# Sigmoid attention with two feed-forward layers: the last 64 keys of two pairs of heads as four 64x64 products

## The chip, the cores and the metric

One core of a Trainium2 chip runs the program. The metric is the time of one execution on the device in microseconds (us). TensorE is called PE below and its weight loads PEld; VectorE is DVE, ScalarE ACT, GpSimd POOL, SyncE SP.

## What is computed

```python
def _attn_ref(q, k, v):                      # 4 batches, 12 heads, 448 positions, 64 per head, float32
    scores = np.matmul(q, k.transpose(0, 1, 3, 2)) / np.sqrt(64) - np.log(448)
    return np.matmul(1.0 / (1.0 + np.exp(-scores)), v)
# x = heads joined: 1792 rows of 768
def _moe_ref(x, w_gate, w_val, w_out, rms_g):   # d_ff 1536
    xn = x / np.sqrt(np.mean(x * x, axis=-1, keepdims=True) + 1e-06) * rms_g
    g = xn @ w_gate
    return g / (1.0 + np.exp(-g)) * (xn @ w_val) @ w_out
def _moe2_ref(x, w_in, w_out):                  # d_ff 2048
    h = x @ w_in
    return (h - np.tanh(h)) @ w_out
```

There is no softmax: each score goes through a sigmoid by itself, so keys can be handled in chunks in any order.

## The kernel before

**Attention.** The 48 heads are worked on as 24 pairs (`b`, `p`): the two heads of a pair lie on partitions 0 to 63 and 64 to 127. The 448 keys of a pair are cut into chunks of 128, 128, 96 and 96 (`rows_of`, `LAST` = 96). For each chunk and head, a product of 64 rows by the chunk's keys by 448 queries gives scores in a PSUM bank (`scores`, L771, plain float32, in the first two pairs; `split_scores`, L751, in the other 22, where q and k are split into a high and a low part by `split_qk` and each product is made of three). ACT takes the sigmoid of each bank (L778). Then `pair_av` (L801) multiplies values by sigmoids: one product per chunk and head, both heads into the two halves of one bank, float32. `pair_end` copies that bank and squares it for the norm. A plain float32 product stands twice in the trace, since it is two instructions there.

**Loads.** `pair_load` fetches a pair's q and k by SP's queue (L694, and two pieces of 64 rows for the last 64 keys, L699, in batches 0 and 1) and v by POOL's or SP's queue (L706, four pieces in batches 0 and 1, three in 2 and 3). Pairs are loaded three ahead.

**Feed-forward.** After attention come the products of the two layers (L1133, L1078, L1158): 128x128 weights against 448 columns, most of them by a scheme that makes seven block products out of eight. Weights are converted on ACT and DVE on the way (L439, L511, L522), partly during attention, and partial sums are added in DRAM (L956).

**What sets the order.** Each piece of work is put on record by `add` with its engines, its costs and the tiles it reads and writes. `Plan.lay` then lays all pieces out: among those that could start soonest by the planner's costs it takes the one with the lowest rank in `ORDER`, a table of numbers, one per piece. Work of one stream ("attention", "moe", "norm") keeps its own order on PE. Buffers come from pools whose sizes stand in `Plan(...)`; PSUM has 8 banks ("at" for scores, up to 2 "av" for values). At the very start PE runs `N_WARM` products of zeros (L446) before its first real one.

Of the kernel before, what the change touches and what calls it, by code (L numbers as in the profile page):

```python
# [244 lines left out]
0bw0aJ0OG1J61Od0kW1LG1vP0000g12UZ0tR1Ts35c17J1Zr0Bn2nY1Wy2OF25P1lm1M01012RL05315n0ou0hJ0aK0jP19B18p1EC0lE1He0nC0Yf0zx0Ck
1Rt1NH20500N0yJ0Dk09O09C0kR24g0Me2FM2B61SX0nw08s04V1J10JK0VG0xW00016D2bp0cI1n-0BK2Bv0570Cy0001p41y_0UI19F0v-1qc1qQ1UD1jS
1aZ0Ws1e80000ra0001Te1pa00016X0000Oq21s27y2zJ1ZZ0xU1AZ1gH0es0Ht1p80K10S40v80uf0Fp0I418v2gN1qX24K2F12v111e2KU28g20H0Z40Jy
0Ft03-15r03c0gr0bG1Kr1w42CI18b0J40cM0fs1Oz0000m80Qa1911h51cX1lz1nt1PT1xA2e91T62721uW1wo0tW0vf00M0va05S0FB2fQ3t_2uM1dw1oM
0qD24G1Bl11x22S1GL3iy20Y3nC1Mr19j1Pa2Tm1ih3NK2DH2ou1Gr20A0ud02u3Pz1Ba2TC3343151ao29v0Mm26D01e0xj2y33lP2rD1iU34Z4Aa1-B1wx
30m2ni3ZA2IL2w922w0z31xL1Ip1BN1G-29r2mz2zc2yW0iI21O2hq2bX2-l3Df1XP1pI1Hw2E52Du2T70in1e03lt1_M2nB1f61vf2jg0_R0xf49Z2pU2MD  # L250
1sX2B52Q32E-2VN1en12v1Qk1wF1x02bh2vd2oD24k0qm0YO0cy0zA0kH1mS1zb3Fj2yE3PC2nn38k2rm2fd1Wp1Vp17M1Pv2kQ2KF3MU2-Y3Bj2St37z1vS
3GT3fP2En1XF11001l07x0Q43FU2s63mp42f3KJ1y02921n02b12wD2ke0vO06K0Qj01l1Rt3XV3P32ub4G64kj2Tl30H2L41s_2Ft0yM3iF4Oe42C1kh1vq
3xd2aV0Al0pi15p1eQ0vr0i91_W01l11Z57u5Iu3eW2va3Fv3hh22A27w2Co2B21y61aT28Y0mx0BQ2bE15I0mn56v4xy3ym4Qx4Fg2CU1mJ1yf2fT38o261
4Tk4tm4HF2Rv34t1em1G90TI1tX2ru1JD5MS2kv4S34i741j4yZ58m2w43062DW1xk33J2LM1RG2JQ3B91dG3f34Ea5CH4Iu2Rv3vD3wP2RC1qs2HM3d33y1
35O56y5Fj3vM2x_3Wz3AA2cn1hs2dx2D52A-2Fi1PN2CC2d30o75V85AR4jb4vD5Vd1tH2CX1vH2Vq2ak3302dA2ls2kr5hI4ye5K630_3k83jT3Z-3Oz5zF
4ja50W54i5DF5-y3po3Py3y12QV2tK2fs1wn2C839s2JF2ZC22H2KC3_J4uI5mQ5QD5XM31A3o04B84zn34f2C02mn2Ii3Iy1zn0cx2gs2bw3pW33q3Pb2_B
33040a2vf3F_2j-3IK2m631m1jS33V2n934z3W23G73K43JV3ME4TQ3Q62lp4uS46F32K3dP3mH3wb4FL4Cu5ti57_3Gm3bh2_-2Nj3PV3HD35d2wY3He4Cv
2_63q14p12nm39-3eB46G3f82zT39B30G3Mp4rU4b15HH5cK3vA4Cw4Vy4id59F5Dm4k053f5WE4Xs4532lB3NX3f146S4LG4W_4Cb3HF6MD4ml61C3NU48A
4BC49a3Tu4dR4dg4uv5cU5Vw4sQ5JN3xn4NP4Ce5BF5Lc6WP4Wd4ySAUT61o5zG2_p4e92093k14jE6HI5I24it4cr57s5FE3sV5yp3ph4nw4zQ5-y5Zk4B7
4oi5O75Yt5L957X5-c4f44yG51F4xx5eh4wM4oq5n85bq5qp67p5DO5oG4Q-5SM4VZ4zF5Wh4ru4S-3Hz4x36C65kL62P7In5c06ga5kR5Ny4NQ4Tb4bM6ZL  # L260
5_u6pQ4sj5MK51c50b5hG7M25cW6q45ln5Ba4lhBRP5WV55r5Eb5-v5dw5yr5916jF6Oz5G36S95Hz6aH6W55q06vl6534ss68d6K_5_z6bi6Jj78u6pp6zj
6fs6QQ7g24vb6AV7Fq6mJ5ky78g6cG6qW5vS6XC7MT7Ft6se7oD5qf7Ks6NF62y56b51p6uB6M_6RO7C_6rm6Fm6c57dd80t4Wu6iH8566pA7bN7PQ7is6zS
6nL7Wq8Ok7967217ma6mK7Gr73s7io6pO7sj8tI7iT7RQ7oo7Cm5xB7td73V8VJ6Xg72T7Kc8IK6-s6-F74g7qM9Sv8n68eq6_E76i7rj6_18b96Rl7nb8KU
7-r7ji8Bs8pX7zc85e8c675B7HY97E66U78l8lI7Mh6fm8aZ8uD7za9O39h88Af6kj6nd5yQ6uw8Po8Cw6cS8it7Od7Hq89y7g39FJ9qz7Vi7Aq7lf7xI6wW
# [1117 lines left out]
```

## Time and profile before

| what | value |
| --- | --- |
| median of 3 runs | 1048.71 us (1043.16 to 1049.61) |
| profiled execution | 1046.03 us |
| its span in the profile | 1044.3 us |
| PE busy | 1031.6 us, 99% of the span |
| ACT busy, DVE busy | 687.3 us, 793.4 us |
| bytes moved | 245.68 MB |

The span is what the profiler saw between the first and the last instruction; 1.7 us of the execution lie around it. PE's busy time is that of pipelined products whose ends are modelled, so 99% says that PE nearly always had work, not that it worked at its peak.

### The profile page before, as it was taken

What the parts mean: (1) busy time and instruction counts of PE and PEld (TensorE: products, weight loads), DVE (VectorE), ACT (ScalarE), POOL (GpSimd) and SP (SyncE); (2) the same over time, 40 slices, a digit from 0 to 9 for tenths busy, and PEclk for the clock granted to TensorE, in tenths of its full rate; (3) what the DMA queues carried; (4) which work ended last, traced back from release to release, by engine and by line L of the source; (5) the groups of instructions that cost most, each with busy time, mean ns of one, the idle gap of its engine ahead of it and who ended that gap; (6) DMA issues with size and microseconds to landing.
All of it is one profiled execution on the core that took longest, in us unless ns stands there. A gap on an engine that the chain in (4) does not pass through costs nothing.

```text
span 1044.3 us, 15612 instructions
## 1 busy us (share of the span) xinstructions
PE 1031.6 (99%) x5324; PEld 888.3 (85%) x5324; DVE 793.4 (76%) x1287; ACT 687.3 (66%) x1260; POOL 163.4 (16%) x234
## 2 busy tenths in 40 slices
PE   8999999999999999999999999999999999999998
PEld 3555558999999989999999989999898899999997
DVE  2858988886977996976755866998797878676866
ACT  5877875685775655775663666678575767675742
POOL 4433000000003142201003030000303300003030
PEclk9999999999999999999999999999999999999999
DMA  7897847866959999979549498485959883649492
GB/s 238 287 346 246 298 150 239 302 224 232 305 166 273 326 259 371 326 291 361 169 115 265 148 214 273 162 306 220 234 178 251 262 212 104 229 135 212 124 251 110
DMA packets 102480, 245.68 MB, mean 235 GB/s; under 512 B 16640, under 2 KB 56992, under 8 KB 102400
## 3 DMA queue, kind: packets, MB, share of 16 engines
q1 hardware_dynamic: 77232, 177.23, 49.8%
q0 software_dynamic: 24864, 67.35, 26.1%
q8 instruction: 42, 0.69, 0.3%
q14 instruction: 38, 0.31, 0.1%
q10 hardware_dynamic: 304, 0.10, 0.0%
HBM read 151.44 MB, written 93.19 MB: 234 GB/s over the span
## 4 chain that ended last, share of the span: by engine, by line
PE 85%; issue 9%; DMA 3%; POOL 1%; DVE 1%; ACT 0%; SPq 0%; POOLq 0%; ACTq 0%
PE ps L1133 43%; PE ps L1078 23%; PE ps L801 7%; PE ps L751 5%; PE ps L1158 5%; POOL out L956 1%; DMA out<-unit 1%; DMA part<-in_vp 1%; DMA part<-in_qkt 1%; PE ps L861 0%; PE ps L836 0%; ACT unit L439 0%; DVE part L522 0%; SPq L699 0%; DVE unit L1014 0%
## 5 line engine op out<-in xcount | busy, mean ns | idle before, releaser
L1133 PE MATMUL ps<-unit,part 128*128 128x448 f32 x2520 | 520.2, 365 | 2.4 <-ACT unit L439 2.3
L1133 PEld LDWEIGHTS ps<-unit,part 128*128 128x128 f32 x2520 | 471.4, 187 | 44.4 <-ACT unit L439 4.6
L1078 PE MATMUL ps<-unit,part 128*128 128x448 f32 x1512 | 311.9, 364 | 1.7 <-ACT unit L439 1.2
L1078 PEld LDWEIGHTS ps<-unit,part 128*128 128x128 f32 x1512 | 283.3, 187 | 24.7 <-ACT unit L439 1.5
L522 DVE TENSOR_TENSOR part<-part 128x768 fp32r<-128x768 f32 (+1 forms) x244 | 214.9, 889 | 68.1 <-ACT part L439 59.3
L439 ACT COPY unit<-ps 128x448 f32<-128x448 f32 x297 | 154.0, 536 | 142.3 <-PE ps L1133 44.8
L439 ACT CAST part<-part 128x768 fp32r<-128x768 f32 (+1 forms) x236 | 182.7, 787 | 21.7 <-DVE part L522 5.8
L885 DVE TENSOR_TENSOR unit<-unit 128x448 fp32r<-128x448 f32 x252 | 152.0, 619 | 45.9 <-ACT unit L439 34.4
L439 ACT CAST unit<-unit 128x448 fp32r<-128x448 f32 x254 | 138.8, 568 | 44.8 <-DVE unit L997 15.5
L1014 DVE TENSOR_TENSOR unit<-ps,unit 128x448 f32<-128x448 f32 x168 | 103.7, 621 | 42.8 <-PE ps L1133 21.1
L890 DVE TENSOR_TENSOR unit<-unit 128x448 f32<-128x448 f32 x144 | 86.0, 618 | 12.6 <-DMA unit<-sumB 8.4
L778 ACT ACTIVATE unit<-ps 128x448 f32<-128x448 f32 (+1 forms) x192 | 86.4, 551 | 8.2 <-PE ps L751 4.4
L956 POOL DMA_DIRECT2D sumB<-unit x48 | 42.4, 945 | 289.5 <-DVE unit L1014 210.3
L801 PE MATMUL ps<-unit,part 128*64 128x448 f32 (+1 forms) x384 | 78.7, 546 | 1.4 <-issue 1.1
L511 DVE SCALAR_TENSOR_TENSOR part<-raw,zero 128x768 uint32<-128x768 uint32 x68 | 64.7, 952 | 12.3 <-ACT zero L439 11.7
L439 ACT CAST zero<-raw 128x768 f16<-128x768 bf16 x52 | 56.1, 1078 | 15.0 <-DVE part L511 5.3
L751 PEld LDWEIGHTS ps<-unit 64*128 64x128 f32 (+1 forms) x528 | 45.0, 171 | 22.2 <-issue 15.3
L801 PEld LDWEIGHTS ps<-unit,part 128*64 128x64 f32 (+1 forms) x384 | 25.2, 136 | 42.2 <-issue 32.5
L1158 PE MATMUL ps<-unit,part 128*128 128x448 f32 x288 | 60.3, 365 | 0.7 <-DVE unit L942 0.3
L751 PE MATMUL ps<-unit 64*128 64x448 f32 (+1 forms) x528 | 60.0, 370 | 0.7 <-DVE unit L439 0.7
L956 POOL DMA_DIRECT2D out<-unit x36 | 31.7, 1092 | 177.3 <-DVE unit L1014 163.3
L1158 PEld LDWEIGHTS ps<-unit,part 128*128 128x128 f32 x288 | 53.7, 188 | 6.3 <-DVE unit L942 1.2
(51 smaller groups left out, 487.6 us busy)
## 6 DMA issues: line engine op xcount, KB each, us to landing
raw<-in_w_out POOLq DMA_DIRECT2D x28, 768.0 KB, 7.9
part<-wD SPq DMA_DIRECT2D x56, 384.0 KB, 5.5
part<-wB SPq DMA_DIRECT2D x36, 384.0 KB, 5.4
wC<-part SPq DMA_DIRECT2D x36, 384.0 KB, 4.7
part<-wC SPq DMA_DIRECT2D x36, 384.0 KB, 3.7
raw<-in_w_in SPq DMA_DIRECT2D x16, 768.0 KB, 7.4
sumB<-unit POOLq DMA_DIRECT2D x48, 224.0 KB, 7.7
wD<-part POOLq DMA_DIRECT2D x28, 384.0 KB, 7.8
```

Of the source, the lines that this page charges most:

```text
L439: add(engines, lambda e: (nc.scalar.copy if e == "ACT" else nc.vector.tensor_copy)(to(), of()), reads, writes)
L522: add({**dve(n, psum=False), **pool(n)}, lambda e: ENG[e].tensor_sub(lo(), of(), hi().bitcast(F32)), [*reads, *kh], [*kl])
L751: nc.tensor.matmul(ps[i, c].tile[:n, :S], lhsT=parts[w].tile[rows, at:at + n], rhs=parts[x].tile[rows, :S], start=q == 0, stop=q == 2)
L778: add(act(S, psum=True), lambda e: nc.scalar.activation(to.tile[at:at + n, :S], ps.tile[:n, :S], AF.Sigmoid, bias=-math.log(S), scale=1.0 ...
L801: nc.tensor.matmul(ps.tile[i * D:(i + 1) * D, :S], lhsT=v.tile[:n, c, i, :] if b < PAIRED else v.tile[:n, i, c, :], rhs=a[c][i].tile[:n, : ...
L885: add({**pool(S), **dve(S, psum=False)}, lambda e: ENG[e].tensor_sub(t["l"].tile, of.tile, t["h"].tile.bitcast(F32)), [of["t"], kh], [kl])
L890: add({**dve(S, psum=False), **pool(S)}, lambda e: ENG[e].tensor_sub(t.tile, x.tile, y.tile), [x["t"], y["t"]], [t["t"]])
L956: add(queue("POOL", True), lambda e: nc.gpsimd.dma_start(out=d.tile, in_=t.tile, accum_op=ALU.add), [t["t"], d["t"]], [d["t"]], moved=move ...
L1014: add(dve(S), lambda e: nc.vector.tensor_add(t.tile, ps.tile[:, :S], t.tile), [ps["t"], t["t"]], [t["t"]])
L1078: nc.tensor.matmul(ps.tile[:, :S], lhsT=part(a), rhs=x[b].tile, start=n in (1, 5) and kp == 0 and q == 0, stop=kp == n_kp - 1 and q == 2, ...
L1133: nc.tensor.matmul(ps.tile[:, :S], lhsT=part(a), rhs=x[b].tile, start=n in ((1, 2, 5) if opening else (1, 5)) and i == 0 and q == 0, stop= ...
L1158: nc.tensor.matmul(ps.tile[:, :S], lhsT=wt, rhs=a[p].tile, start=start and i == 0, stop=stop and i == 2, skip_group_check=True)
```

## The change

The keys are cut into 128, 128, 128 and 64. The three whole chunks go as before (`chunk_scores`, `pair_av`). The last 64 keys of two pairs of heads, four heads, are done together: `tail_scores` makes four products of 64 rows by 64 keys, each in a quarter of PE's array of its own (two row halves by two column halves), into two banks; two sigmoids take these; `tail_av` makes the four 64x64 products of sigmoids and values. The tails are plain float32 in all pairs, not split. A tail's scores stand ahead of the two pairs' other scores, and its values ahead of their other values, so that two "av" banks are open together. `pair_load` makes three transfers a pair (q, k, v), five for the odd pairs of batches 0 and 1, and loads four to five pairs ahead. `N_WARM` goes from 16 to 6. Pool sizes change, and `ORDER` is another table. In the diff the removed lines of functions that are printed above are left out.

```diff
@@ -30,12 +30,12 @@
 PLAIN_SETS = {("B", 0): (2,), ("D", 0): (), ("B", 1): (2,), ("D", 1): ()}
 NQK = S + 4 * P
-LAST = S // 2 - P
+MAIN = S // P
 PAIRED = 2
 SPLIT_QK = (0, 1, 2, 3)
 WHOLE_QK = 2
 HP = H // 2
-N_WARM = 16
+N_WARM = 6
 MM, MM_96 = 203, 190
 SOON = 100
 HELD = 3
@@ -238,127 +238,125 @@
 ORDER = """
-00000000009Q09T00000B0Hv0470000000000000KW04c0mi0DX0Jj01t0470Ih0a10OZ0YV0_0WBFV-c0000PA0Mg1040N802c0Qk05x0Dg0631T50uO1V4
...
-VgQXNrWQ8YMHUlTXZGXeK
+XTM00005G02F0qs09o0L400003D0En1Bv0a50bS0lk0AK0uq0O3XUQXsS0KJ0Og0xM0YP07-1OS0Ja0D915Y0Id0A301415k0R31mU0l40JJ0mI0U11QE0eg
...
 """
@@ -391,10 +389,10 @@
     dram_p = ctx.enter_context(tc.tile_pool(name="spill", bufs=1, space=DRAM))
     plan = Plan({
-        "unit": (N_UNIT, {"moe": N_MOE, "s": 18, "acc": 6, "accs": 12, "st": 4, "sum": 6, "x": 16, "xr": 4, "tmp_m": 8, "tmp_a": 4, "sq": 3, "rstd": 2,
+        "unit": (N_UNIT, {"moe": N_MOE, "s": 22, "acc": 6, "accs": 9, "st": 4, "sum": 6, "x": 16, "xr": 4, "tmp_m": 10, "tmp_a": 4, "sq": 3, "rstd": 2,
                           "xs": 42, "tmp_s": 9, "tmp_x": 4, "qk": 12}),
         "raw": (N_RAW, {"raw": N_RAW}),
-        "part": (N_PART, {"cv": 3, "again": 4, "vs": 4, "qkr": 6, "whl": 6, "op": 8}),
+        "part": (N_PART, {"cv": 4, "again": 4, "vs": 6, "qkr": 10, "whl": 8, "op": 8}),
         "ps": (8, {"mm": 6, "at": 8, "av": 2, "nm": 1, "m2": 8}),
     })
     add = plan.add
@@ -685,125 +683,134 @@
     xs, sqs, rcs, rstd, spilled = {}, {}, {}, {}, {}
     def pair_load(b, p):
...
+        tq, tk, v = qkr_t[b, p] = part_of("qkr", [P, S]), part_of("qkr", [P, 4 * P]), part_of("vs", [P, 4, 2, D] if b < PAIRED else [P, 2, 4, D])
+        vs_t[b, p] = v
         both = qkt[b * H + 2 * p:b * H + 2 * p + 2].rearrange("h r c -> (h r) c")[D:D + P]
...
+        by = "POOL" if b < PAIRED else "SP"
+        def part(e, to, of, key, size, packets=P):
+            add({e: (540 if e == "POOL" else 620, False)}, lambda e: ENG[e].dma_start(out=to(), in_=of), [], [key], moved=moved(size, packets))
+        part("SP", lambda: tq.tile, both[:, :S], tq[0], 4 * S)
+        end = 4 * P if b < PAIRED else S
+        cuts = (0, P, end) if (b, p) == (0, 0) else (0, end)
+        for n, (lo, hi) in enumerate(zip(cuts, cuts[1:])):
+            part("ACT" if hi == P else "SP", lambda lo=lo, hi=hi: tk.tile[:, lo:hi], both[:, S + lo:S + hi], tk[n], 4 * (hi - lo))
+        if b >= PAIRED:
+            part(by, lambda: v.tile, vt[(b - PAIRED) * H + 2 * p:][:2].rearrange("i p c d -> p i c d"), v[0], 1024, 2 * P)
+            return
+        of = vp[b * HP + p]
+        n = 3 + (p % 2 == 0)
+        part(by, lambda: v.tile[:, :n], of[:, :n], v[0], 512 * n)
+        for i in range(2 * (p % 2)):
+            part(by, lambda i=i: v.tile[HEADS[1 - i], 3, i], of[HEADS[i], 3, i], v[1 + i], 256, D)
+    HEADS = [slice(i * D, (i + 1) * D) for i in range(2)]
+    def k_of(t, b, c, i):
+        at = MAIN * P + i * D * (b < PAIRED) if c == MAIN else c * P
+        return t.tile[HEADS[i], at:at + (D if c == MAIN else P)]
+    def v_of(t, b, c, i):
+        return t.tile[:, c, i] if b < PAIRED else t.tile[:, i, c]
     qk_t = {}
     def split_qk(b, p):
...
+        tq, tk, _ = qkr_t[b, p]
+        for x, t, n in (("q", tq, S), ("k", tk, MAIN * P)):
             h, l = unit("qk", F32R), unit("qk", F32R)
             qk_t[b, p, x + "h"], qk_t[b, p, x + "l"] = h, l
...
+            of = lambda t=t, n=n: t.tile[:, :n]
+            copy({**act(n), **dve(n, fast=True)}, lambda h=h, n=n: h.tile[:, :n], of, [t[0]], [h["t"]])
+            add(dve(n, psum=False), lambda e, h=h, l=l, of=of, n=n: nc.vector.tensor_sub(l.tile[:, :n], of(), h.tile[:, :n].bitcast(F32)), [t[0], h["t"]], [l["t"]])
     def is_split(b, p):
         return b in SPLIT_QK and b * HP + p >= WHOLE_QK
...
+    def scores(*which):
+        for n, x in enumerate(which):
+            chunk_scores(*x, 75 * (n == 0))
+    def chunk_scores(b, p, c, more):
+        ps = [bank("at") for _ in range(2)]
+        tq, tk, _ = qkr_t[b, p]
+        if is_split(b, p):
+            qk = {x: qk_t[b, p, x] for x in ("qh", "ql", "kh", "kl")}
+            reads = [x["t"] for x in qk.values()]
+            terms = [(qk[w], qk[x]) for w, x in (("kh", "qh"), ("kh", "ql"), ("kl", "qh"))]
+        else:
+            reads = [tq[0], tk[0], *[tk[1]] * (b == p == 0 and c > 0)]
+            terms = [(tk, tq)]
         def run(e):
...
+            for q, (w, x) in enumerate(terms):
+                for i, rows in enumerate(HEADS):
+                    nc.tensor.matmul(ps[i].tile[:, :S], lhsT=k_of(w, b, c, i), rhs=x.tile[rows, :S],
+                                     start=q == 0, stop=q == len(terms) - 1)
+        add({"PE": ((3 * MM if len(terms) > 1 else 750) + more, False)}, run, reads, [x["t"] for x in ps], stream="attention")
+        for i in range(2):
+            t = a_t[b, p, c, i] = unit("s")
+            sigmoid(ps[i], t)
+    def sigmoid(ps, to):
+        add(act(S, psum=True), lambda e: nc.scalar.activation(
+            to.tile, ps.tile[:, :S], AF.Sigmoid, bias=-math.log(S), scale=1.0 / math.sqrt(D)), [ps["t"]], [to["t"]])
+    def tail_scores(b, p):
+        ps = [bank("at") for _ in range(2)]
+        raw = [qkr_t[b, p + o] for o in range(2)]
         def run(e):
...
+            for o in range(2):
+                tq, tk, _ = raw[o]
+                for i, rows in enumerate(HEADS):
+                    nc.tensor.matmul(ps[o].tile[HEADS[i ^ o], :S], lhsT=k_of(tk, b, MAIN, i), rhs=tq.tile[rows, :], start=True, stop=True)
+        add({"PE": (750 + 75, False)}, run, [x for tq, tk, _ in raw for x in (tq[0], tk[0], *[tk[1]] * (tk is qkr_t[0, 0][1]))],
+            [x["t"] for x in ps], stream="attention")
+        for o in range(2):
+            t = a_t[b, p + o, MAIN] = unit("s")
+            sigmoid(ps[o], t)
+    def tail_av(b, p):
+        opened = (b, p) in av_t
+        ps = [av_t[b, p + o] if opened else bank("av") for o in range(2)]
+        a, v = [a_t.pop((b, p + o, MAIN)) for o in range(2)], [vs_t[b, p + o] for o in range(2)]
+        for o in range(2):
+            av_t[b, p + o] = ps[o]
+        def run(e):
+            for o in range(2):
                 for i in range(2):
...
+                    rows = HEADS[i ^ o]
+                    nc.tensor.matmul(ps[o].tile[HEADS[i], :S], lhsT=v_of(v[o], b, MAIN, i)[rows], rhs=a[o].tile[rows, :],
+                                     start=not opened, stop=opened, skip_group_check=True)
+        add({"PE": (750 + 75, False)}, run, [*(x["t"] for x in a), v[0][0], *(v[1][x] for x in range(3 if b < PAIRED else 1))], [x["t"] for x in ps], stream="attention")
     def pair_av(b, p):
...
+        opens = (b, p) not in av_t
+        if opens:
+            av_t[b, p] = bank("av")
+        ps, v = av_t[b, p], vs_t[b, p]
+        a = [[a_t.pop((b, p, c, i)) for i in range(2)] for c in range(MAIN)]
         def run(e, cs):
             for c in cs:
...
                 for i in range(2):
...
+                    nc.tensor.matmul(ps.tile[HEADS[i], :S], lhsT=v_of(v, b, c, i), rhs=a[c][i].tile,
+                                     start=opens and c == 0, stop=not opens and c == MAIN - 1, skip_group_check=True)
+        for cs in ((0, 1), (2,)):
+            add({"PE": (2 * len(cs) * 375 + 75, False)}, lambda e, cs=cs: run(e, cs),
+                [v[0], *[x["t"] for c in cs for x in a[c]]], [ps["t"]], stream="attention")
     def pair_end(b, p):
         ps = av_t.pop((b, p))
@@ -1207,13 +1214,24 @@
     def attn_units(b):
         units = []
...
+        value = lambda at: (pair_av(*pairs[at]), pair_end(*pairs[at]))
+        for at in range(b * HP, (b + 1) * HP, 2):
+            one, two = pairs[at:at + 2]
+            q_of = lambda x, *cs: lambda: scores(*((*x, c) for c in cs))
+            tail = lambda one=one: tail_scores(*one)
+            old_tail = lambda at=at: tail_av(*pairs[at - 2])
+            ready = [lambda at=at: (get_ready(at + 4), ready_split(at + 1)), lambda at=at: (get_ready(at + 5), ready_split(at + 2))]
+            olds = [lambda at=at, o=o: value(at - 2 + o) for o in range(2)]
+            if at == 0:
+                units += [ready[0], q_of(one, 0), q_of(one, 1, 2), ready[1], q_of(two, 0, 1, 2), tail, lambda: pair_av(*pairs[0])]
+            elif at == 2:
+                units += [ready[0], q_of(one, 0), lambda: pair_av(*pairs[1]), q_of(one, 1, 2), ready[1], tail, old_tail,
+                          lambda: (pair_end(*pairs[0]), pair_end(*pairs[1])), q_of(two, 0, 1, 2)]
+            else:
+                units += [tail, old_tail, ready[0], q_of(one, 0), olds[0], q_of(one, 1, 2), ready[1], olds[1], q_of(two, 0, 1, 2)]
         if b == B - 1:
...
+            at = len(pairs)
+            units += [lambda: tail_av(*pairs[at - 2]), lambda: value(at - 2), lambda: value(at - 1)]
         return units
     nc.gpsimd.memset(mark, 0.0)
@@ -1226,7 +1244,7 @@
     nc.gpsimd.memset(expo, -0.5)
-    for p in range(3):
+    for p in range(4):
         pair_load(0, p)
     add({"SP": (100, False)}, lambda e: nc.sync.dma_start(out=g_sb, in_=rms_g))
     add({"SP": (100, False)}, lambda e: nc.sync.dma_start(out=id_sb, in_=ident))
@@ -1252,13 +1270,15 @@
         return [lambda u=u: run(u) for u in units]
+    OPENING = 8
     def mixed(units, *others):
         at = [0] * len(others)
-        for u in units[:2]:
+        for u in units[:OPENING]:
             u()
-        units = units[2:]
+        units = units[OPENING:]
         for n, u in enumerate(units):
             u()
             for k, o in enumerate(others):
```

PE at the start of the program, before: the last of the 16 products of zeros, then the first pairs of heads (L771 plain scores, L801 values, L751 split scores).

```order
L446 MATMUL ps<-mark 128x448
L771 MATMUL ps<-part 128x448 x4
L771 MATMUL ps<-part 96x448 x4
L771 MATMUL ps<-part 128x448 x4
L801 MATMUL ps<-unit,part 64x448 x8
L771 MATMUL ps<-part 96x448 x4
L751 MATMUL ps<-unit 128x448 x12
L801 MATMUL ps<-unit,part 64x448 x8
L751 MATMUL ps<-unit 96x448 x12
```

The same place of the change: L444 zeros, L751 the whole chunks' scores, L772 and L792 scores and values of a tail, L808 the whole chunks' values.

```order
L444 MATMUL ps<-mark 128x448
L751 MATMUL ps<-part 128x448 x12
L772 MATMUL ps<-part 64x448 x4
L808 MATMUL ps<-unit,part 64x448 x6
L751 MATMUL ps<-unit 128x448 x6
L808 MATMUL ps<-unit,part 64x448 x6
L751 MATMUL ps<-unit 128x448 x12
L772 MATMUL ps<-part 64x448 x4
L792 MATMUL ps<-unit,part 64x448 x4
L751 MATMUL ps<-unit 128x448 x18
```

Both of the first pairs' scores now come ahead of any values, and six products a pair stand where eight stood, with four tail products for two pairs.

PE in batch 1, before, around the norm of batch 0 (L836 sums, L446 clearing a bank):

```order
L801 MATMUL ps<-unit,part 64x448 x8
L751 MATMUL ps<-unit 96x448 x12
L751 MATMUL ps<-unit 128x448 x12
L801 MATMUL ps<-unit,part 64x448 x4
L836 MATMUL ps<-ones,unit 112x1 x4
L801 MATMUL ps<-unit,part 64x448 x4
L446 LDWEIGHTS mark
L446 MATMUL ps<-mark 128x448
```

The same place of the change (L843 sums, L444 clearing):

```order
L772 MATMUL ps<-part 64x448 x4
L792 MATMUL ps<-unit,part 64x448 x4
L751 MATMUL ps<-unit 128x448 x6
L808 MATMUL ps<-unit,part 64x448 x6
L843 MATMUL ps<-ones,unit 112x1 x4
L751 MATMUL ps<-unit 128x448 x12
L808 MATMUL ps<-unit,part 64x448 x6
L444 LDWEIGHTS mark
L444 MATMUL ps<-mark 128x448
L751 MATMUL ps<-unit 128x448 x18
```

Before, two pairs were four runs of products on PE: scores (24 instructions), values, scores, values. Now they are seven: tail scores, tail values, scores of one chunk, values, scores of two chunks, values, scores of three chunks.

SP's queue at the start, before (L694 q and k, L699 their last 64 keys, L706 v):

```order
L694 DMA part<-in_qkt 128x448
L694 DMA part<-in_qkt 128x256
L706 DMA part<-in_vp 128x384
L694 DMA part<-in_qkt 128x448
L694 DMA part<-in_qkt 128x384
L699 DMA part<-in_qkt 64x64 x2
L706 DMA part<-in_vp 32x128
L706 DMA part<-in_vp 64x64
```

The same place of the change, where L692 stands for every transfer of `pair_load`:

```order
L692 DMA part<-in_qkt 128x448
L692 DMA part<-in_qkt 128x384
L692 DMA part<-in_qkt 128x448
L692 DMA part<-in_qkt 128x512
L692 DMA part<-in_qkt 128x448
```

SP no longer carries v in batch 0, and no piece of 64 rows stands between two pairs' q and k.

## Rows read from the trace of the kernel before

**Rows 1.** Chain that ended last, attention: start us, us, what xcount.

```profile
29.32 2.60 PE ps L751 x24
31.93 3.16 PE ps L801 x16
35.09 2.60 PE ps L751 x24
...
72.35 1.66 PE ps L801 x8
74.01 0.88 PE ps L836 x8
...
137.90 1.39 PE ps L751 x12
```

**Rows 2.** The same chain, feed-forward: the first long run and the last.

```profile
166.33 52.79 PE ps L1133 x261
...
1016.80 23.67 PE ps L1078 x117
```

**Rows 3.** Groups by line: engine op out<-in, shape, xcount | busy us, mean ns.

```profile
L1133 PE MATMUL ps<-unit,part 128*128 128x448 f32 x2520 | 520.2, 365 | 2.4 <-ACT unit L439 2.3
L1078 PE MATMUL ps<-unit,part 128*128 128x448 f32 x1512 | 311.9, 364 | 1.7 <-ACT unit L439 1.2
L778 ACT ACTIVATE unit<-ps 128x448 f32<-128x448 f32 (+1 forms) x192 | 86.4, 551 | 8.2 <-PE ps L751 4.4
L801 PE MATMUL ps<-unit,part 128*64 128x448 f32 (+1 forms) x384 | 78.7, 546 | 1.4 <-issue 1.1
L1158 PE MATMUL ps<-unit,part 128*128 128x448 f32 x288 | 60.3, 365 | 0.7 <-DVE unit L942 0.3
L751 PE MATMUL ps<-unit 64*128 64x448 f32 (+1 forms) x528 | 60.0, 370 | 0.7 <-DVE unit L439 0.7
```

**Rows 4.** Timeline of weight loads at the start: start us, us, xcount [idle before].

```profile
1.94 0.13 PEld L446 LDWEIGHTS <-mark 128*128 128x128 bf16 x2 [1.94 <-POOL mark L1219]
2.29 0.15 PEld L446 LDWEIGHTS <-mark 128*128 128x128 bf16 x1 [0.22 <-issue]
2.66 0.15 PEld L446 LDWEIGHTS <-mark 128*128 128x128 bf16 x1 [0.22 <-issue]
...
4.90 1.34 PEld L446 LDWEIGHTS <-mark 128*128 128x128 bf16 x7 [0.22 <-issue]
6.62 0.30 PEld L771 LDWEIGHTS ps<-part 64*128 64x128 f32 x4 [0.37 <-PE ps L446]
```

**Rows 5.** Chain that ended last, transfers and waits of the start.

```profile
0.74 2.79 DMA part<-in_qkt
...
10.34 8.38 DMA part<-in_vp
...
21.34 1.13 issue
...
23.53 2.63 PE ps L751 x23
```

**Rows 6.** Windows: us, PE busy (x) PEld DVE ACT POOL busy (x), PEclk, DMA share, GB/s.

```profile
1.90:4.90 3.00, 2.96 (x8) 1.19 (x9) 0.00 (x0) 1.49 (x2) 3.00 (x8) 1.00 0.84 210
14.50:16.90 2.40, 1.74 (x10) 0.57 (x8) 0.47 (x2) 2.23 (x5) 0.00 (x0) 1.00 1.00 342
16.90:18.80 1.90, 1.66 (x12) 1.01 (x12) 0.55 (x1) 1.39 (x4) 0.56 (x1) 1.00 1.04 369
18.80:23.50 4.70, 3.51 (x18) 1.28 (x18) 2.14 (x5) 1.05 (x3) 0.51 (x1) 1.00 0.65 188
60.00:80.00 20.00, 20.00 (x141) 10.96 (x140) 12.36 (x25) 16.23 (x37) 3.46 (x5) 1.00 0.96 342
100.00:120.00 20.00, 20.00 (x135) 10.45 (x136) 18.26 (x35) 16.77 (x38) 2.79 (x5) 1.00 0.86 284
160.00:180.00 20.00, 20.00 (x105) 17.77 (x102) 16.65 (x29) 11.19 (x17) 1.01 (x1) 1.00 0.81 274
```

More of the change, by code (lines that the diff above doesn't have):

```diff
@@ L245 @@
[L245 to L264, printed above, removed]
@@ L362 @@
+XpEbdfamuXPqaLmb8bZARbA7ZmgcFvYKrZ_jaWIZ3vYx_WCGcguYdXaclbmscVzYuZa54XkYcg_YdzbAXa7_bZtb2aZnkcmAbD8ch6YnxYBFWuO
 """
@@ L696, in pair_load @@
-        if b < PAIRED:
-            for i in range(2):
-                rows, at = slice(i * D, (i + 1) * D), S + 3 * P + i * D
-                add({"ACT" if first else "SP": (620, False)}, lambda e, rows=rows, at=at: ENG[e].dma_start(
-                    out=tk.tile[rows, 3 * P:], in_=both[rows, at:at + D]), [], [tk[2 + i]], moved=moved(256, D))
-        v = vs_t[b, p] = part_of("vs", [P, 4, 2, D] if b < PAIRED else [P, 2, 4, D])
-        by = "POOL" if 0 < b < PAIRED or b == 0 and p > 1 else "SP"
@@ L736, in is_split @@
     def is_split(b, p):
         return b in SPLIT_QK and b * HP + p >= WHOLE_QK
-    def split_scores(b, p, cs):
-        ps = {(i, c): bank("at") for c in cs for i in range(2)}
-        parts = {x: qk_t[b, p, x] for x in ("qh", "ql", "kh", "kl")}
-        def run(e):
-            for c in cs:
-                n = rows_of(c)
-                at = c * P - (P - LAST) * (c == 3)
-                for q, (w, x) in enumerate((("kh", "qh"), ("kh", "ql"), ("kl", "qh"))):
-                    for i in range(2):
-                        rows = slice(i * D, (i + 1) * D)
-                        nc.tensor.matmul(ps[i, c].tile[:n, :S], lhsT=parts[w].tile[rows, at:at + n], rhs=parts[x].tile[rows, :S],
-                                         start=q == 0, stop=q == 2)
-        add({"PE": (sum(3 * (MM) for c in cs) + 75, False)}, run,
-            [x["t"] for x in parts.values()], [x["t"] for x in ps.values()], stream="attention")
-        return ps
@@ L758, in scores @@
-    def scores(b, p, cs):
-        if is_split(b, p):
-            return split_scores(b, p, cs)
-        tq, tk = qkr_t[b, p]
-        ps = {(i, c): bank("at") for c in cs for i in range(2)}
-        def run(e):
-            for c in cs:
-                n = rows_of(c)
-                for i in range(2):
-                    rows = slice(i * D, (i + 1) * D)
-                    at = c * P - (P - LAST) * (c == 3)
-                    nc.tensor.matmul(ps[i, c].tile[:n, :S], lhsT=tk.tile[rows, at:at + n], rhs=tq.tile[rows, :], start=True, stop=True)
-        parts = [0] + [1] * ((b, p) == (0, 0) and cs[-1] > 0) + [2, 3] * (b < PAIRED and cs[-1] == 3)
-        add({"PE": (2 * len(cs) * 375 + 150, False)}, run, [tq[0], *(tk[x] for x in parts)], [x["t"] for x in ps.values()], stream="attention")
-        return ps
@@ L804, in pair_av @@
-        for cs in ((0, 1), (2, 3)):
-            add({"PE": (4 * 375 + 75, False)}, lambda e, cs=cs: run(e, cs),
-                [*(v[x] for x in range(2 if cs[-1] < 3 else 6)), *[x["t"] for c in cs for x in a[c]]], [ps["t"]], stream="attention")
+                    nc.tensor.matmul(ps.tile[HEADS[i], :S], lhsT=v_of(v, b, c, i), rhs=a[c][i].tile,
[3 more added lines that the diff above has]
+                [v[0], *[x["t"] for c in cs for x in a[c]]], [ps["t"]], stream="attention")
```

266 lines of the change are left out of this document (117 added, 149 removed).

## The prediction, made before the changed kernel was run

> **What bounds the kernel now.** I read the windows first, to see which engine is short of time in each part. During attention PE has no idle time in any 20 us window after the start, while ACT is busy for 16.2 to 16.8 us of 20 and DVE for 12.4 to 18.3; in the feed-forward part PE is full as well, its weight loads too (17.8 of 20) [rows 6]. The chain that ended last says the same in order of time: from 23.5 us on it is PE all the way through attention, one pair of heads after another, 2.60 us of scores and 3.16 us of values each, and then long runs of feed-forward products [rows 1, 2, 5]. So a product taken from attention's PE stream shortens the program, unless something else is late next. Before 23.5 us it is different: the chain runs through transfers of q, k and v [rows 5], and PE has gaps [rows 6].
>
> What is left to gain in the feed-forward part is little. A product there takes 52.79 / 261 = 0.202 us [rows 2], and there are 2520 + 1512 + 288 = 4320 of them [rows 3], 45 of which lie inside attention, before 166.33. 4275 x 0.2023 = 864.8 us, while the stretch from 166.33 to the end of the last run at 1016.80 + 23.67 = 1040.47 is 874.1. So at most 9.3 us of it are not products.
>
> **The price of attention's products.** A run of 24 split-score instructions takes 2.60 us, one of 12 takes 1.39 [rows 1]: 1.21 us for 12 more, so 0.101 us each and 0.18 us for starting the run. They are two heads on two halves of the array: 24 x 0.202 would be 4.8 us if they ran one by one, so they run in twos, at 0.202 for two. A run of 16 value instructions takes 3.16, one of 8 takes 1.66 [rows 1]: 1.50 for 8 more, 0.376 for two heads' instructions (one step) and 0.15 for the start. The start is what PE pays for going from one shape of product to another.
>
> **The split pairs, two at a time (11 of the 12 twos).** Before: 2 x (2.60 + 3.16) = 11.52 us. After, scores: three runs of 6, 12 and 18 instructions, 36 x 0.101 + 3 x 0.18 = 4.17. Values: two runs of 6 steps, 12 x 0.376 + 2 x 0.15 = 4.81. Tails: scores and values are four float32 products each, twice that in instructions, in four quarters of the array. If four run abreast as two do now, each is 2 steps, 0.75 us; both are of one shape and follow each other, so one start: 4 x 0.376 + 0.15 = 1.65. Sum 10.63, that is 0.89 less, and 11 x 0.89 = 9.8 us. If the second tail pays a start too, it is 0.15 more, 8.1 in all. I take 9.8. No row of before shows a 64x64 product. By the nearest rows, two abreast, a tail is 4 steps instead of 2: 24 tails x 2 x 0.376 = 18.0 us more. That end stays in the range.
>
> **The first two pairs**, plain float32: 32 steps before, 12 + 2 + 12 + 2 = 28 after, 4 x 0.376 = 1.5, less one more start: 1.4 us.
>
> **The start.** Sixteen products of zeros run from 1.94 us, spaced 0.37 us until 4.90 and faster after it, and the first real product comes at 6.62, after waiting for PE [rows 4]. The granted clock reads 1.00 throughout [rows 6], but 448 columns in 0.37 us are the 1.2 GHz level. Six of them end at 1.94 + 6 x 0.37 = 4.2, so up to 2.4 us are gained if q and k are there: q's transfer lands at 0.74 + 2.79 = 3.53 [rows 5]. The real products between 4.2 and 4.9 then run at the lower level and lose about 0.4. I take 2.0, between 0 (data late, or the level rises later without the zeros) and 2.4.
>
> PE's gaps in the three windows from 14.5 to 23.5 are 0.66, 0.24 and 1.19 us [rows 6], 2.1 together, and the chain there is a transfer of v that took 8.4 us and an issue gap [rows 5]. After, SP carries q and k without the small pieces and is no longer the queue of any v in batch 0, so each later q, k and v is issued sooner. I take 1.2 of the 2.1, between a gain of 2.1 and a loss of 2.1 (the DMA engines are at 1.00 to 1.04 there already, and the weights' loads come earlier on POOL).
>
> **Work on ACT and PSUM.** Seven sigmoids a pair instead of eight: 24 x 0.45 = 10.8 us less for ACT (86.4 us for 192) [rows 3]. ACT is not the bound, so I count nothing. But the last six banks of scores are now made in 1.8 us, with two more for a tail right behind, while ACT needs 0.45 us a bank, 3.6 for eight. With two banks held for values, six are left, so the tail's scores may wait for a sigmoid, behind which all of PE stands: 0 to one sigmoid, 0.45, at each of 12 places, 0 to 5.4 us. I take 1.0, near the low end, since ACT has idle time in every window.
>
> **DVE, DMA and the feed-forward part.** k's split is 384 columns wide instead of 448, a little less for DVE. The transfers are fewer (about 85 instead of 157 for q, k and v) of about the same bytes. The feed-forward part has the same products; its table of ranks is new. I count 0, between minus 9.3 (all that is not products gone) and plus 9.3 (as much again).
>
> **Sum.** 9.8 + 1.4 + 2.0 + 1.2 - 1.0 = 13.4 us, from the profiled execution's 1046.03 (span 1044.3 and 1.7 around it): 1032.6. The median of the runs shown is 2.7 higher; the profiled one lies among the three. I say 1033.
>
> **Rivals.**
>
> Tails two abreast. The four products of a tail write two banks, each bank from both row halves of the array. Nothing in the trace has this: scores now write one bank from one row half each, and values write one bank from both column halves, with all rows. If the second row half has to wait, a tail takes 4 steps, 18.0 us more in all, and with the extra starts the program goes to 1032.6 + 18.0 = 1050.6, slower than before. It decides from 13.4 / 24 = 0.56 us more a tail, 1.31 instead of 0.75 us. For it speaks that no row shows four; against it, that both ways of halving the array run two abreast now at full rate [rows 1], and the two products that share columns go to different banks. The Trainium skill's page TensorEngine Tiling (Array Packing), Restrictions and Gotchas, says that different row tiles cannot access the same PSUM bank simultaneously; by that rule, read to the letter, this rival is the outcome, while no run here shows it yet. In full sequence a tail would be 8 steps: 24 x 6 x 0.376 = 54 us more, 1087.
>
> The gain is given back at the entry to the feed-forward part. It starts 13 us earlier, and its first weights must be converted by then. For it: DVE is busy for 16.7 to 18.3 of 20 us around there [rows 6], and the same conversions get less time. Against: ACT is at 11.2 of 20 from 160 to 180, and DVE has 7.6 us of 20 idle from 60 to 80, where work can go earlier [rows 6]. PE would wait up to what was gained in the split pairs, 9.8 us: 1042.
>
> The start doesn't follow: with few products of zeros and data late, the start gains nothing or loses 2: 1036 to 1038, less than 1% with it.
>
> **How the numbers follow.** One per cent of 1048.7, 10.5 us, is about what a measurement of this kernel can tell from no change; faster by more is below 1038.2. The forecast, four abreast and PE still the bound, with the start's and the banks' bounds, is 1024 to 1038: 0.63. Gain partly given back at the entry or the start, 1038 to 1046: 0.21. Tails two abreast, about 1050, within 1%: 0.10. Slower by more, in sequence or two abreast with new waits in the feed-forward part: 0.06. So faster 0.63, same 0.31, slower 0.06. The range of 8 in 10 leaves out the low edge and most of the last two: 1024 to 1048.
>
> **What would show it.** The chain through attention should have twos of about 10.6 us, with tails of 0.75 us a run, L772 and L792; 1.5 us there means two abreast. The first L751 should start near 4.2 us. Attention's last values should end about 13 us earlier, and the run of feed-forward products behind them should have no gap. ACT's sigmoids should be 168. Wrong would be: tails at 1.3 us or more; PE waiting for ACT's sigmoids ahead of L772 by more than 0.1 us each; PE waiting for DVE or ACT conversions between 150 and 220 us.

## The result, and the profile after

The changed kernel takes 1036.76 us (median of 6 runs, 1035.92 to 1040.15), the one before, measured beside it, 1048.41 (6 runs). The ratio is 0.990 (95% interval 0.9876 to 0.9925): faster by 1.0%, 3.8 us above the 1033.0 predicted and inside the range. Its profiled execution took 1035.96 us, with a span of 1034.2, 10.1 less than before.

First PE's timeline over one two (two pairs of heads): start us, us to the modelled end, form, count. Starts are what to subtract, since ends overlap the next start.

```profile
22.40 0.98 PE L772 MATMUL ps<-part 64*64 64x448 f32 x8
23.20 0.93 PE L792 MATMUL ps<-unit,part 64*64 64x448 f32 x8
24.07 0.87 PE L751 MATMUL ps<-unit 64*128 64x448 f32 x6
24.87 2.48 PE L808 MATMUL ps<-unit,part 128*64 128x448 f32 x12
27.27 1.49 PE L751 MATMUL ps<-unit 64*128 64x448 f32 x12
28.69 2.48 PE L808 MATMUL ps<-unit,part 128*64 128x448 f32 x12
31.09 2.11 PE L751 MATMUL ps<-unit 64*128 64x448 f32 x18
33.14 0.98 PE L772 MATMUL ps<-part 64*64 64x448 f32 x8
```

A tail's scores hold PE for 23.20 - 22.40 = 0.80 us, its values for 24.07 - 23.20 = 0.87: two steps of 0.376 and 0.05 and 0.12 for starting. So four products run abreast. This two takes 33.14 - 22.40 = 10.74. Before it was 2 x (35.09 - 29.32) = 11.54 by the starts in [rows 1]; 10.63 was predicted.

The start, same view:

```profile
1.94 2.42 PE L444 MATMUL ps<-mark 128*128 128x448 bf16 x6 [1.94 <-POOL mark L1237]
4.29 3.26 PE L751 MATMUL ps<-part 64*128 64x448 f32 x12
8.33 2.53 PE L751 MATMUL ps<-part 64*128 64x448 f32 x12 [0.78 <-DMA part<-in_qkt]
10.78 0.98 PE L772 MATMUL ps<-part 64*64 64x448 f32 x8
```

The first product comes at 4.29, as predicted. But PE then waits 0.78 us for the second pair's q and k. As many score instructions of before, in its PE timeline:

```profile
6.62 4.78 PE L771 MATMUL ps<-part 64*128 64x448 f32 x24
11.33 3.23 PE L801 MATMUL ps<-unit,part 128*64 128x448 f32 x16
```

There they need no wait, and end (by the next start) at 11.33, in after at 10.78.

Windows of the same stretches as [rows 6], with one more, 98:107 (us, busy us and count of PE, PEld, DVE, ACT, POOL, granted clock, DMA share, GB/s):

```profile
14.50:16.90 2.40, 2.40 (x18) 0.87 (x14) 1.58 (x2) 0.98 (x2) 0.00 (x0) 1.00 1.04 382
16.90:18.80 1.90, 1.90 (x20) 1.14 (x20) 1.00 (x3) 0.59 (x2) 0.00 (x0) 1.00 1.05 334
18.80:23.50 4.70, 4.70 (x46) 2.55 (x50) 4.67 (x9) 4.34 (x11) 3.30 (x6) 1.00 1.05 387
98.00:107.00 9.00, 8.44 (x52) 3.58 (x48) 9.00 (x18) 6.73 (x16) 1.08 (x2) 1.00 0.77 230
100.00:120.00 20.00, 19.44 (x126) 9.08 (x128) 19.94 (x41) 18.74 (x43) 0.00 (x0) 1.00 0.53 169
```

The gaps from 14.5 to 23.5 are gone. New is a shortage from 98 on: DVE is busy for all of 98:107 and ACT for 18.74 of 20. The chain that ended last names its source:

```profile
88.60 8.85 DMA wB<-part
...
97.55 0.96 DVE part L509
98.51 1.19 DVE unit L938 x2
99.70 0.55 DVE unit L897
100.27 1.01 ACT unit L437 x2
101.32 1.32 PE ps L751 x6
...
158.56 49.15 PE ps L1140 x243
...
477.31 9.09 DMA part<-wAv
...
486.41 0.63 DVE unit L1021
...
487.08 38.22 PE ps L1140 x180
```

A store of a converted weight to DRAM took 8.85 us to land, and DVE's next conversion (L509), which needs the store's buffer, waited 6.5 us for it. Behind it DVE and ACT have more to do than time: PE waits 0.54 us for ACT just before 101.32, and the products behind that stand wide apart (six in 1.32 us, where a run of six takes 0.80). In the feed-forward part stands a wait that before doesn't have, for the load of wAv.

Feed-forward's products are the same in number and length as in [rows 3], and ACT's sigmoids are 168 (groups by line: busy us, mean ns):

```profile
L1140 PE MATMUL ps<-unit,part 128*128 128x448 f32 x2520 | 521.4, 365 | 4.5 <-DVE unit L1021 3.8 <-ACT unit L437 0.6
...
L760 ACT ACTIVATE unit<-ps 128x448 f32<-128x448 f32 x168 | 79.1, 567 | 15.5 <-PE ps L751 15.3
```

**Where the 10.1 us come from.** The first long run of feed-forward products starts at 158.56 instead of 166.33 [rows 2], and 63 instead of 45 such products already lie inside attention: 7.77 + 18 x 0.2023 = 11.4 us gained by then. The rest of the program gives 10.1 - 11.4 = -1.3. That is not an even loss. The chain of before has this run at the place where after waits for wAv:

```profile
483.95 47.32 PE ps L1133 x234
```

It ends at 531.27. The same 234 products end at 487.08 + 38.22 = 525.30 in after, so only 6.0 us are left there, and 10.1 - 6.0 = 4.1 come back behind it.

### The profile page after: what moved, and what is told of

The parts are those of the page before. It is cut to its first block, busy times and chain, and to the rows that moved or that the text cites. A ratio compares the mean times of both kernels' runs of the same rounds, so it can differ in the third digit from the quotient of the medians.

```text
span 1034.2 us, 15346 instructions
## 1 busy us (share of the span) xinstructions
PE 1022.0 (99%) x5270; PEld 878.2 (85%) x5270; DVE 789.6 (76%) x1288; ACT 679.4 (66%) x1235; POOL 155.8 (15%) x218
## 4 chain that ended last, share of the span: by engine, by line
PE 88%; DMA 2%; DVE 1%; issue 1%; POOL 0%; ACT 0%; POOLq 0%; DVEq 0%
PE ps L1140 49%; PE ps L1085 30%; PE ps L1165 5%; PE ps L808 2%; PE ps L751 1%; DMA part<-wAv 1%; DMA wB<-part 1%; PE ps L792 0%; PE ps L772 0%; POOL rc L849 0%; DVE part L509 0%; DVE part L573 0%; PE ps L843 0%; ACT unit L437 0%; PE ps L868 0%
## 5 line engine op out<-in xcount | busy, mean ns | idle before, releaser
L437 ACT CAST unit<-unit 128x448 fp32r<-128x448 f32 x257 | 140.8, 568 | 44.2 <-DVE unit L1004 14.5
L760 ACT ACTIVATE unit<-ps 128x448 f32<-128x448 f32 x168 | 79.1, 567 | 15.5 <-PE ps L751 15.3
L509 DVE SCALAR_TENSOR_TENSOR part<-raw,zero 128x768 uint32<-128x768 uint32 x68 | 64.9, 955 | 21.9 <-ACT zero L437 12.3
L808 PE MATMUL ps<-unit,part 128*64 128x448 f32 x288 | 59.4, 548 | 0.0
L751 PEld LDWEIGHTS ps<-unit 64*128 64x128 f32 x396 | 34.8, 184 | 25.5 <-ACT unit L760 12.1
L751 PE MATMUL ps<-unit 64*128 64x448 f32 x396 | 50.5, 381 | 0.6 <-ACT unit L437 0.5
L808 PEld LDWEIGHTS ps<-unit,part 128*64 128x64 f32 x288 | 18.5, 136 | 30.0 <-issue 29.1
```

The lines of the kernel that those rows point to most:

```text
L437: add(engines, lambda e: (nc.scalar.copy if e == "ACT" else nc.vector.tensor_copy)(to(), of()), reads, writes)
L751: nc.tensor.matmul(ps[i].tile[:, :S], lhsT=k_of(w, b, c, i), rhs=x.tile[rows, :S], start=q == 0, stop=q == len(terms) - 1)
L760: add(act(S, psum=True), lambda e: nc.scalar.activation(to.tile, ps.tile[:, :S], AF.Sigmoid, bias=-math.log(S), scale=1.0 / math.sqrt(D)), ...
L808: nc.tensor.matmul(ps.tile[HEADS[i], :S], lhsT=v_of(v, b, c, i), rhs=a[c][i].tile, start=opens and c == 0, stop=not opens and c == MAIN - ...
```

## The experiments

**The changed kernel again.**

> The changed kernel once more, beside the others on the same chip. By its earlier runs its ratio to the kernel before is 0.988 to 0.993, some 10 us less.

Measured: 1035.67 us, ratio 0.9886 (0.9869 to 0.9902). PE's wait for wAv was 4.2 us and ended at 487.7. A third time (e10, below) gave 1036.0.

**Tails on two quarters of the array.** Both pairs' products of a tail go to the same two quarters, and the small pieces of v are laid to match.

```diff
-            part(by, lambda i=i: v.tile[HEADS[1 - i], 3, i], ...
+            part(by, lambda i=i: v.tile[HEADS[i], 3, i], ...
-  nc.tensor.matmul(ps[o].tile[HEADS[i ^ o], :S], lhsT=k_of(tk, b, MAIN, i), ...
+  nc.tensor.matmul(ps[o].tile[HEADS[i], :S], lhsT=k_of(tk, b, MAIN, i), ...
-                    rows = HEADS[i ^ o]
+                    rows = HEADS[i]
```

> The tails' four products use two quarters of the array instead of four (the second pair's on the same quarters as the first's); nothing else moves. Theory, four quarters run abreast: a tail run goes from 0.80 us to 1.5 to 1.6, and the whole is 24 x 0.75 = 18 us longer than the changed kernel, 16 if the few tails that wait for ACT hide it: slower than the kernel before by 6 to 8 us. Rival, the four products were never abreast or the run is limited by issuing instructions: 0 to 3 us.

Measured: 1051.4 us, ratio 1.0034 (1.0021 to 1.0046), 15.7 above e0. PE's timeline of this kernel:

```profile
36.06 1.72 PE L772 MATMUL ps<-part 64*64 64x448 f32 x8
37.61 1.67 PE L792 MATMUL ps<-unit,part 64*64 64x448 f32 x8
39.21 0.87 PE L751 MATMUL ps<-unit 64*128 64x448 f32 x6
```

A run of tail products now takes 1.55 and 1.60 us. With two abreast the change is slower than before: that the four quarters work together is what the whole gain hangs on. It is also the measured price of the first rival, 1050.6 in the prediction.

**Sixteen products of zeros again.**

```diff
-N_WARM = 6
+N_WARM = 16
```

> Sixteen products of zeros at the start instead of six, all else as changed. Theory, what ends the start is the second pair's q and k (PE waits for them from 7.0 to 8.3 us in the changed kernel): the first real product moves from 4.3 to 6.6 us, but the second pair's scores only from 8.3 to about 9.0, so 0.5 to 1.0 us longer. Rival, the prediction's term: 2.0 us longer.

Measured: 1038.41 us, ratio 0.9909 (0.9891 to 0.9927), 2.7 above e0. The trace doesn't bear out that the zeros cost that. The first product came at 7.24 and the first tail at 11.95, 1.2 later than in after; but the long run of feed-forward products started at 157.59, 1.0 earlier, because the shortage at 101 us was smaller. PE's wait for wAv was 5.9 us, and the run behind it was longer than in e0, where it took 38.23:

```profile
488.78 39.27 PE ps L1140 x180
```

The granted clock read 0.50 from 488 to 494. In the profiled executions 1.7 us more of waiting and 1.0 more of this run, less 1.0 at the entry, make nearly all of the 1.9 by which the span is longer. Why the wait was longer no run shows. The theory fell, and the rival's sum came near by another way.

**Six products of zeros in the kernel before** (`N_WARM = 6`).

> The kernel before with six products of zeros instead of sixteen. Theory, its start is set by the transfer of v that lands at 18.7 us: the first product comes at 4.3 instead of 6.6 us, but the values of the second pair still wait, so 0 to 0.5 us less in all. Rival, the products of zeros are on the path: 2.0 us less.

Measured: 1046.93 us, ratio 0.9998 (0.9987 to 1.0008), as the theory had it. PE's timeline of this kernel:

```profile
4.29 5.71 PE L771 MATMUL ps<-part 64*128 64x448 f32 x24
9.93 3.23 PE L801 MATMUL ps<-unit,part 128*64 128x448 f32 x16
...
16.62 1.65 PE L751 MATMUL ps<-unit 64*128 64x448 f32 x12 [1.78 <-DVE unit L439]
18.57 2.48 PE L801 MATMUL ps<-unit,part 128*64 128x448 f32 x12 [0.30 <-DMA part<-in_vp]
```

The earlier start ends in a longer wait at 16.62 (0.69 us in before), for DVE's splitting of q and k, which itself waited 3.9 us, until 16.08, for their transfer: there the transfers decide, not PE.

**Short stores of wB**, the weights converted during attention.

```diff
+    for (ph, _), d in whole_w.items():
+        d.short = ph == "B"
-        ... dma_start(out=d.tile[:, at], in_=c.tile) ...
+        n = P if by == "POOL" and d.short else NW
+        ... dma_start(out=d.tile[:, at, :n], in_=c.tile[:, :n]) ...
```

> The converted weights of the first layer's output (wB) are stored 128 of 768 columns wide, and their reload reads these columns six times, so that layer multiplies by part of its weights. Same order, a sixth of these stores' bytes. Theory: PE's slow stretch from 99 to 117 us in the changed kernel begins with DVE idle for 6.5 us until a wB store lands at 97.5, behind which DVE's and ACT's work queues up; without it PE has no wait there, and the long run of feed-forward products that began at 158.5 us begins some 3 us earlier. Rival: ACT and DVE have too much work in that stretch whatever the store does (18.7 and 19.9 us busy of 20): it begins less than 1 us earlier.

Measured: 1038.41 us, ratio 0.992 (0.9893 to 0.9947). The long run started at 156.21, 2.35 earlier than in after, and PE had no wait from 98 to 107 us:

```profile
98.00:107.00 9.00, 9.00 (x64) 3.95 (x60) 7.76 (x16) 8.37 (x19) 0.00 (x0) 1.00 0.64 213
```

So the wait for the landing store is the cause of the shortage. The end doesn't show it (1038.41 us, above e0's 1035.67): PE waited 8.0 us in later stages (4.2 for DVE's L1027, 3.8 for ACT), where this kernel's reads in small pieces may play a part. What 2.35 us are worth at the end has to come from another run.

**Short stores of wD**, those under way near 480 us (the same edit with `"D"`).

> The same with the stores of the second layer's output weights (wD), first layer's as changed; the second layer multiplies by part of its weights. Theory: the wait of PE for 3.8 us that ends at 487 us, with the lower clock after it, comes from reloads of wAv that wait for buffers of wD stores (SP waited 11.3 us for these) and share full DMA engines with them: with short stores the wait falls under 1.5 us, the clock stays up, and 4 to 5.6 us are gained there. Rival: the reloads are late because SP issues them behind a load that waits for DVE: the wait stays above 3 us.

Measured: 1028.88 us, ratio 0.9824 (0.9798 to 0.9851), 6.8 below e0 (6.5 by the ratios, since e4 to e7 were measured beside other runs of before than e0). The chain of this kernel:

```profile
471.78 47.32 PE ps L1146 x234
```

234 products follow each other without a break where after stands still, as the theory had it. So the stores of wD make the wait. Whether they do it by their share of the DMA engines or by the buffers they hold, for which SP's loads wait (11.3 us from 455 to 495 in after, 5.3 here), this run doesn't separate. In e10, the changed kernel again (below), the chain ends the same wait with such a store, and not with wAv:

```profile
479.28 7.79 DMA wD<-part
```

**One more part buffer in the changed kernel.**

```diff
-N_UNIT, N_MOE, N_RAW, N_PART = 72, 40, 2, 20
+N_UNIT, N_MOE, N_RAW, N_PART = 72, 40, 2, 21
```

> The changed kernel with 21 buffers in the pool of weight and q, k, v parts instead of 20. The planner's order moves a little, for it sees the buffer. Theory: the buffer wait behind the reloads of wAv goes, no PE wait of over 1.5 us near 487 us, 4 to 5 us less than the changed kernel, about 1031. Rival: the wait is DMA's load and not the buffer: within 1 us of the changed kernel, or slower by another wait that the other order brings.

Measured: 1032.84 us, ratio 0.9862 (0.9836 to 0.9888). The long run starts at 155.79 and the shortage at 98 us is gone. Near 482 PE waits 0.6 us, under the 1.5 of the theory, but this order has a wait of 2.5 us for ACT between 790 and 820 us. The gain is 2.8 us to e0, less than expected.

**One more part buffer in the kernel before** (the same edit).

> The kernel before with 21 buffers in the same pool. If the wait for wAv belongs to the changed kernel's table alone, the kernel before has nothing to gain: within 2 us of it. If a buffer more helps any order: 4 us less.

Measured: 1051.44 us, ratio 1.0044 (1.0025 to 1.0063): 4.9 slower than the kernel before, measured beside it. Neither expectation held. A buffer more is no gain by itself; it changes the whole order.

**Short stores of wD in the kernel before.**

> The kernel before, with each store of a converted wD tile cut to its first 128 columns (of 768), and read back six times over; so the part of wD beyond the first 128 columns is left out of what is computed. It is the control for e5, where the same cut gave the changed kernel 6.8 us. Theory (the wait for the load of wAv near 481 us is the changed order's own, made by its transfers meeting there): the kernel before has no such wait, and gains 0 to 2 us, 1046 to 1048. Rival (any order gains when the transfers carry this much less): 5 to 7 us, 1040 to 1043.

Measured: 1045.38 us, ratio 0.9979 (0.9966 to 0.9992), 2.0 less than the kernel before. This is the top of the theory's range, and far from the rival's. The wait that e5 took away belongs to the changed order.

**The part buffer, and the changed kernel, side by side.**

> The changed kernel with 21 part buffers again, beside the changed kernel itself in the same call. If e6's gain is real: 1031 to 1034, 2 to 4 us below the changed kernel, and the whole 95% interval of its ratio below that kernel's. If e6 was luck of one chip: the two overlap.

> The changed kernel beside e9 and e8, in the same call: 1035 to 1038, ratio 0.988 to 0.991, with PE's wait of about 4 us for the load of wAv that ends near 487 us.

Measured: 1031.9 us, ratio 0.9847 (0.9827 to 0.9867), beside 1036.0, ratio 0.9885 (0.9869 to 0.9902): 4.1 us, with intervals that just don't touch. With one buffer more the change is 1.5% faster than before, and faster than as it was made. PE's timeline in e9, where the order holds the same products:

```profile
90.38 0.98 PE L772 MATMUL ps<-part 64*64 64x448 f32 x8
102.23 0.98 PE L772 MATMUL ps<-part 64*64 64x448 f32 x8
112.97 0.98 PE L772 MATMUL ps<-part 64*64 64x448 f32 x8
```

and in after:

```profile
90.10 0.98 PE L772 MATMUL ps<-part 64*64 64x448 f32 x8
103.91 1.48 PE L772 MATMUL ps<-part 64*64 64x448 f32 x8
115.26 0.98 PE L772 MATMUL ps<-part 64*64 64x448 f32 x8
```

The two cycles take 11.85 + 10.74 in e9 (the first holds work of the norm, too) and 13.81 + 11.35 in after: the shortage costs 2.6 us at this place. That the 4.1 come from there isn't shown: in e9 the wait near 482 us is shorter, too, 1.1 us, and the clock stays up behind it.

e10 is the program of after, and yet its shortage is larger. The same two cycles take 14.19 + 12.72 us, and the long run starts at 160.67, 2.1 later than in after. Its span is 1034.2 all the same, for PE's wait near 487 is 3.3 us instead of 3.8 and the clock stays up behind it, so that the run of 180 products ends at 525.36. What PE gained or lost ahead of that wait was thus swallowed by it here, and in e2, which came earlier and waited longer.

**Sixteen zeros beside the part buffer.** Both edits above, `N_PART` 21 and `N_WARM` 16.

> The changed kernel with 21 part buffers (as e6 and e9, in which PE has no wait between 98 and 107 us) and again 16 products of zeros instead of 6. Theory (the ten zeros cost the 1.2 to 1.4 us that e2 showed at the start, and e2's stretch up to the long run of feed-forward products swallowed it only because PE waits at 101 us for work that doesn't depend on the start): with that wait gone the delay stays, the tail scores near 33 us start at 34.2 to 34.8, the long run at 157.0 to 157.6 (156.0 in e6 and e9 on average), and the total is 1 to 2 us above theirs, 1033 to 1034.5. Rival (the delay is taken up by slack somewhere else in attention): the long run at 155.8 to 156.3 in spite of a later start, and 1032 to 1033.

Measured: 1032.52 us, ratio 0.9844 (0.983 to 0.9858); the long run at 156.56 (155.79 in e6, 156.24 in e9), the tail scores near 33 us at 33.73. Neither expectation holds whole: the delay stays, but it is 0.3 to 0.8 us and not seen in the total. PE's timeline of this kernel tells why it is smaller than in e2:

```profile
1.94 4.78 PE L444 MATMUL ps<-mark 128*128 128x448 bf16 x16 [1.94 <-POOL mark L1237]
6.64 4.78 PE L751 MATMUL ps<-part 64*128 64x448 f32 x24
11.36 0.98 PE L772 MATMUL ps<-part 64*64 64x448 f32 x8
```

Here the zeros took 6.64 - 1.94 = 4.70 us, in e2 5.30 for the same sixteen: their spacing went from 0.37 us to half of it after 5.2 us here and after 6.4 there. What the zeros cost differs from execution to execution.

## Why the prediction was right, and where not

The forecast held: PE is the bound, the tails run four abreast, and the time fell by about what was predicted. Of the 13.4 us forecast, 11.4 came in attention. That the total came near is partly luck, as the last paragraph of this section shows. By the prediction's own terms, in us:

| term | predicted | measured | from |
| --- | --- | --- | --- |
| eleven split twos | 9.8 | 8.8 | 11 x (11.54 - 10.74) |
| first two pairs | 1.4 | not by itself | |
| zeros | 2.0 | 0.55 | 11.33 - 10.78 |
| gaps, 14.5 to 23.5 | 1.2 | 2.1 | windows |
| PE waiting for banks, sigmoids | -1.0 | -2.6 | after against e9 |
| feed-forward | 0 | -1.3 | 10.1 - 11.4 |
| sum, and total measured | 13.4 | 10.1 | spans |

With 1.4 for the first two pairs the attention terms make 10.25 of the 11.4 measured. The other 1.15 no run pins down; before cuts its last values and scores into more runs than after, which would each pay a start, but this wasn't tried.

**Tails.** The step "2 steps, 0.75 us" was right, and 1.65 us for both became 1.67. The two as a whole is 0.11 us longer than worked out, most of it in the runs of scores, which take 0.80, 1.42 and 2.05 us where 0.79, 1.39 and 2.00 were taken. The first rival is refuted, with its price confirmed by e1. The Trainium skill's page TensorEngine Tiling (Array Packing), Restrictions and Gotchas, says that different row tiles cannot access the same PSUM bank simultaneously. The trace does not agree: each bank of a tail is written from both row halves, to different partitions, and the four products take 0.80 us where two at a time take 1.55.

**Zeros.** The step "Six of them end at 1.94 + 6 x 0.37 = 4.2, so up to 2.4 us are gained" named the data's lateness as a bound and then took 2.0. The first product did come 2.33 us earlier (4.29 for 6.62). But the 24 instructions that follow took 10.78 - 4.29 = 6.49 us instead of 11.33 - 6.62 = 4.71: 0.78 is the wait for the second pair's q and k, and the other 1.0 is in the main the lower level of the clock, for which 0.4 had been taken. The granted clock reads 1.00 there; it is the spacing that shows the level, 3.26 us for the first 12 instructions and 2.53 for the next 12. In e3, with no wait between them, the 24 take 9.93 - 4.29 = 5.64 us, 0.93 more than 4.71. e2 and e11 put the ten zeros at 1.2 and 0.5 us at the start. These are rough: with six zeros the first tail starts between 10.40 (e0) and 10.90 us (e9). e3 shows that in the old order they hid behind transfers.

**Gaps.** The step that took 1.2 of 2.1 was too careful. All of it came, with the DMA engines at 1.04 to 1.05, as full as before or fuller. So zeros and gaps together gave 2.65 of the 3.2 predicted: the sum was near, its parts were not.

**Banks and sigmoids.** The sign was right, the mechanism wrong. In the steady twos of after no wait for a sigmoid shows in PE's starts: the runs stand where their steps put them. The 2.6 us are lost in one place, where DVE stands behind a store of wB that takes 8.85 us to land; PE's weight loads do wait for sigmoids there (up to 0.7 us), but ACT had itself waited 5.5 us for DVE. The prediction looked at ACT's idle time in each window and never asked which buffers the conversions reuse. e4 takes the wait away by a shorter store, e6 and e9 by one buffer more, and the long run comes 2.3 to 2.8 us earlier than in after each time. How much the shortage costs is a matter of the execution: in e2 the two cycles lose 0.4 us against e9, in e10 4.3.

**Feed-forward.** The entry was right: no gap behind 158.56, and DVE's conversions there are in time, so the second rival failed at its place. Its kind came true 320 us later. At 483.3 PE waits 3.8 us for the load of wAv, and the run behind it takes 38.22 us instead of 180 x 0.2023 = 36.4, because the granted clock fell: 5.6 us together. Against that stand waits of before that are gone. A window of before:

```profile
743.00:751.00 8.00, 5.97 (x30) 5.20 (x28) 3.33 (x6) 3.01 (x7) 1.73 (x2) 1.00 1.09 289
```

and of after:

```profile
743.00:751.00 8.00, 8.00 (x41) 7.42 (x40) 6.53 (x12) 4.55 (x9) 0.00 (x0) 1.00 1.08 324
```

The same stage comes some 10 us earlier in after, and there PE is busy for all of 728 to 752. PE's waits of 2.1, 1.2 and 0.5 us between 743 and 826 in before have become one of 0.6 at 794. The zero taken was the middle of -9.3 to +9.3, and the net came out at -1.3; but it is the sum of -5.4 up to 525.30 and +4.1 behind it, terms that are as large as the change's other parts, and no run ties either to the tails. That they nearly cancel is luck. e5 gives 6.8 us back by carrying less there, while e8 gives the old order 2.0. What the new table of ranks does alone, without the tails, was not tried.

## What to carry to other kernels

Price a run of products by steps and starts, and count how many quarters of the array work at once: 64x64 products are worth having only if four run abreast. When PE's work shrinks, look for the next wait in buffers whose last use is a DMA store, not in the busy shares: a store that landed 8.85 us after its issue held DVE, which was busy for only 5.56 of the 13 us from 85 to 98, and one buffer more was worth 2.8 to 4.1 us here and cost 4.9 in the other order. Don't book a gain at one stage as a gain of the total before you have looked at the next long wait: here 11.4 us at the entry to the feed-forward part were 6.0 behind the wait for wAv. A start that is bound by transfers, as that of before, gains next to nothing from PE being ready earlier (0.5 us in e3).
